# A decode block in one stream of weights: the pair sum and the last four row chunks of the down projection arranged differently

## The chip, the cores and the metric

One Trainium2 chip; the kernel runs on one of its cores. The metric is the device time of one execution in microseconds, the median of several runs. A profile is one profiled execution, in which the span runs from the first to the last instruction of the program.

## The reference

One decode step of a transformer block for 8 sequences: layer norm, attention over a window of W = 1024 cached positions (32 query heads, 4 key heads, head size 128), output projection and residual, then layer norm, a gated feed-forward part with gelu, and residual. All in float32, without casts.

```python
x = A_x                                             # 8 x 1 x 1024
h = x + _A_ref(_layernorm(x), A_k_cache, A_v_cache, A_wq, A_wo)
h2 = h + _B_ref(_layernorm(h), B_w_gate, B_w_up, B_w_down)
...
g = jnp.einsum("bsd,df->bsf", x, w_gate)            # 1024 -> 3584
u = jnp.einsum("bsd,df->bsf", x, w_up)
h = _gelu(g) * u
return jnp.einsum("bsf,fd->bsd", h, w_down)         # 3584 -> 1024
```

The down projection, the last einsum, is what the change touches: 3584 rows are 28 row chunks (q = 0 to 27) of 128 rows and 1024 columns, 512 KB each.

## The kernel before

All weights and the cache windows are laid out by the host as one flat array, in the order in which they are used, and read into one large buffer `w` of 128 partitions by transfers that SyncE issues (`load`, L102 to L104). Each transfer has a semaphore of its own, `loaded[i]`, on which TensorE waits before the first matmul that reads it. A place in `w` is written again when the matmuls that read it are done, so SyncE waits on TensorE's marks ahead of each issue. The list of loads: query weights (0, 1), keys (2, 3), values (4, 5), output weights (6, 7), gate and up weights (8 to 11), then the row chunks of the down projection in parts of 8, 8, 4, 4, 2 and 1 chunks (`DN_PARTS`, loads 12 to 17), and the last chunk 27 in two pieces: the first 192 columns of each quarter of 256 (`CUT`, load `tail`), then the other 64 of each (load `tail + 1`). That last piece, 128 rows of 1 KB, goes out as three transfers of 100, 20 and 8 partitions (`SHARES`, L329 to L331), all counted on one semaphore. All loads from part 3 on are issued in one go when the last up-projection matmul is done (L325 to L331).

Activations are kept transposed: a stationary operand of 128 rows by 32 columns holds the 8 sequences at every fourth column, and TensorE's 128 columns are used as four groups of 32, each of which writes 32 partitions of a PSUM bank. The activated hidden values are `at_[:, q, :]`.

The down projection runs over the row chunks (L357 to L396):

- Chunks 0 to 25 (`pairs`), L364: each is two matmuls of 512 columns. Up to chunk 19 (`SLOW`) they use two of the four groups; from 20 on even and odd chunks take different groups, so that four run side by side. They add up in bank 7, which then holds two halves, each as two partial sums on different partitions.
- VectorE copies bank 7 to `d1` (L371).
- Chunk 26, L378: four quarters of 256 columns, one to each group, in two pieces of 192 and 64 columns that start banks 0 and 1 (`fin`).
- The pair sum, L384: matmuls with the constant `add2` add the two partial sums of `d1` into the same quarters, in the same two pieces, on top of chunk 26.
- Chunk 27, L391: the same for the last chunk, each piece as its load arrives.
- VectorE adds the residual `h_sb` to each piece (L401, L404); SyncE stores the first (L407), ScalarE the second (L409).
- At the end SyncE waits for a count from ScalarE (`s_end`), clears the semaphores and waits for both stores.

The trace lists each float32 matmul twice, so L364 has 104 for 26 chunks of two.

Of the kernel before, what the change touches and what calls it, by code (L numbers as in the profile page):

```python
# [8 lines left out]
P = 128  # L9
B = 8  # L10
D = 1024
HQ, HKV, DH = 32, 4, 128
REP = HQ // HKV
DF = 3584
EPS = 1e-5
NC = D // P
NQ = 4
QW = D // NQ
# [4 lines left out]
GAP = 144  # L23
CUT = 192


ROUND = 3 * N * NC
PLACE = [0, HALF] * 5 + [0, ROUND]
DN_PARTS = (8, 8, 4, 4, 2, 1)
DN_AT = (2 * ROUND, 0, 8 * D, ROUND, ROUND + 4 * D, ROUND + 6 * D)  # L30

SHARES = ((0, 100), (100, 120), (120, 128))
LAST_AT = ROUND + 7 * D

SLOW = 20


class Engine:
# [39 lines left out]
def decode_block(nc, out, x, srcs, W):  # L78
# [3 lines left out]
    def sb(name, shape):  # L82
        return nc.alloc_sbuf_tensor(name, list(shape), F32).ap()

    first = nc.alloc_semaphore("first")
    pe = Engine(nc, nc.tensor, "pe")
    dve = Engine(nc, nc.vector, "dve")
# [4 lines left out]
    s_load = [nc.alloc_semaphore(f"s_load{i}") for i in range(len(srcs))]  # L92
    s_fin = nc.alloc_semaphore("s_fin")
    s_end = nc.alloc_semaphore("s_end")
    s_out = nc.alloc_semaphore("s_out")

    w = sb("w", [P, 2 * HALF])
    loaded = [(s, 16) for s in s_load]
    loaded[-1] = (s_load[-1], 16 * len(SHARES))
    tail = 12 + len(DN_PARTS)  # L100

    def load(i, at, size, *deps):  # L102
        sp.wait(*deps)
        nc.sync.dma_start(w[:, at:at + size], srcs[i]).then_inc(s_load[i], 16)  # L104
# [10 lines left out]
    t = pool(lambda e: e.memset(ident, 0.0))  # L115
# [8 lines left out]
    add2 = sb("add2", [P, 2, 32])  # L124
# [9 lines left out]
    def bank(i, n=1):  # L134
        return banks[:, i * N:(i + n) * N]
# [35 lines left out]
    for hf in range(2):  # L171
        q_ps = bank(4 + hf)
        for c in range(NC):
            for j in range(NQ):
                ins = pe(lambda e: e.matmul(  # L175
                    q_ps[32 * j:32 * j + 32, :], xt[:, c],
                    w[:, hf * HALF + c * SET + j * N:hf * HALF + c * SET + (j + 1) * N],
                    start=(c == 0), stop=(c == NC - 1)), loaded[hf], t_xt, inc=False)
# [3 lines left out]
    for hf in range(2):  # L182
        q_sb = sb(f"q{hf}", [P, N])
        t = dve(lambda e: e.tensor_scalar(q_sb, bank(4 + hf), scale, None, op0=ALU.mult), t_q[hf])  # L184
        qt = sb(f"qt{hf}", [P, N])
        t = dve(lambda e: e.transpose(qt, q_sb), t)
# [7 lines left out]
    t_s, t_p, share, t_share = [], [], [], []  # L194
    p_sb = [sb(f"p{hf}", [P, W]) for hf in range(2)]
    for hf in range(2):
        s_ps = bank(2 * hf, 2)
        k_t = w[:, hf * HALF:(hf + 1) * HALF].rearrange("p (s b k) -> p s b k", s=2, b=B)
        for b in range(HB):
            for k0 in range(0, W, N):  # L200
                for r in range(NQ):
                    s, half = divmod(r, 2)
                    at = 32 * b + 160 * half
                    ins = pe(lambda e: e.matmul(  # L204
                        s_ps[32 * r:32 * r + 32, k0:k0 + N], qz[hf][:, s, at:at + 32],
                        k_t[:, s, half * HB + b, k0:k0 + N],
                        start=(b == 0), stop=(b == HB - 1)), loaded[2 + hf], t_qz[hf], inc=False)
# [3 lines left out]
        t = dve(lambda e: e.tensor_reduce(out=nmax, in_=s_ps, axis=AX.X, op=ALU.max, negate=True), t_s[hf])  # L211
        tot = sb(f"tot{hf}", [P, 1])
        t = act(lambda e: e.activation(p_sb[hf], s_ps, AF.Exp, bias=nmax, accum_out=tot), t)  # L213
        t_p.append(t)
        rtot = sb(f"rtot{hf}", [P, 1])
        t = dve(lambda e: e.reciprocal(rtot, tot), t)
# [4 lines left out]
    t_o, o_sb, t_osb, t_ot = [], [], [], [None, None]  # L221
# [11 lines left out]
    for hf in range(2):  # L233
        pt = sb(f"pt{hf}", [P, KC, P])
        t_pt = []
        for h in range(2):
            pp = bank(6 + h).rearrange("p (c m) -> p c m", m=P)
            for i in range(KC // 2):
                c = h * KC // 2 + i
                ins = pe(lambda e: e.transpose(pp[:, i], p_sb[hf][:, c * P:(c + 1) * P], ident),  # L240
                         t_p[hf], t_id, free[h], inc=False)
            t = pe.mark(ins)
# [8 lines left out]
        for c in range(KC):  # L251
            for r in range(NQ):
                s, half = divmod(r, 2)
                ins = pe(lambda e: e.matmul(  # L254
                    o_ps[32 * r:32 * r + 32, :], pt[:, c, 32 * r:32 * r + 32],
                    v_t[:, s, c, half * HB:(half + 1) * HB, :],
                    start=(c == 0), stop=(c == KC - 1)), loaded[4 + hf], t_pt[2 * c // KC], t_qz[hf], inc=False)
# [3 lines left out]
        t = dve(lambda e: e.tensor_scalar(  # L261
            o_sb[hf], o_ps[:, 0:DH], share[hf][:, 0:1], None, op0=ALU.mult), t_o[hf], t_share[hf])
# [31 lines left out]
    t = pe.mark(ins)  # L294
# [7 lines left out]
    for k, nb in enumerate((NQ, DF // N - NQ)):  # L302
        pair = bank(2 + 2 * k, 2)
        t_g = []
        for s in range(2):
            i = 8 + 2 * k + s
            for c in range(NC):
                for j in range(nb):
                    at = PLACE[i] + (c * nb + j) * N
                    ins = pe(lambda e: e.matmul(  # L310
                        pair[32 * j:32 * j + 32, s * N:(s + 1) * N], ht[:, c], w[:, at:at + N],
                        start=(c == 0), stop=(c == NC - 1)), loaded[i], t_ht, t_p[1], t_osb[1], inc=False)
                if k == 0 and s == 1 and c == NC // 2 - 1:
                    t_half = pe.mark(ins)
            t_g.append(pe.mark(ins))
            if k == 0 and s == 0:
                load(10, PLACE[10], ROUND, t_g[0])
            elif k == 0:
                load(11, PLACE[11], ROUND, t_half)
                load(12, DN_AT[0], DN_PARTS[0] * D, t_g[1])  # L320
            elif s == 0:
                for i in range(1, 3):
                    load(12 + i, DN_AT[i], DN_PARTS[i] * D, t_g[0])
            else:
                for i in range(3, len(DN_PARTS)):  # L325
                    load(12 + i, DN_AT[i], DN_PARTS[i] * D, t_g[1])
                load(tail, LAST_AT, NQ * CUT)
                at = LAST_AT + NQ * CUT
                for p0, p1 in SHARES:  # L329
                    nc.sync.dma_start(w[p0:p1, at:at + D - NQ * CUT], srcs[tail + 1][p0:p1]).then_inc(  # L330
                        s_load[tail + 1], 16)  # L331
        rows = 32 * nb
        ge = sb(f"ge{k}", [P, N])
        t = act(lambda e: e.activation(ge[:rows], pair[:rows, 0:N], AF.Gelu_apprx_tanh), t_g[0])  # L334
        hm = sb(f"hm{k}", [P, N])
        t = dve(lambda e: e.tensor_mul(hm[:rows], ge[:rows], pair[:rows, N:2 * N]), t, t_g[1])  # L336
        if k == 0:
            t_at.append(dve(lambda e: e.transpose(at_[:, 0:16, :].rearrange("p c m -> p (c m)"), hm), t))
        else:
            hp = bank(6)[:, 0:4 * rows].rearrange("p (i m) -> p i m", i=4)  # L340
            for i in range(4):
                ins = pe(lambda e: e.transpose(hp[:, i], hm[:rows, i * P:(i + 1) * P], ident[:rows, :rows]),
                         t, t_ot[0], inc=False)
            t = pe.mark(ins)
            t_at.append(dve(lambda e: e.tensor_copy(
                at_[:, 16:28, :].rearrange("p (j i) m -> p i j m", j=nb),
                hp.rearrange("p i (j m) -> p i j m", j=nb)), t))
# [7 lines left out]
        of += [12 + i] * n  # L355

    d1_ps = bank(7)  # L357
    pairs = DF // P - 2
    started = set()
    for q in range(pairs):  # L360
        for ch in range(2):
            r = ch if q < SLOW else 2 * (q % 2) + ch
            at = where[q][0] + ch * N
            ins = pe(lambda e: e.matmul(  # L364
                d1_ps[32 * r:32 * r + 32, :], at_[:, q, :], w[:, at:at + N],
                start=(r not in started), stop=(q >= pairs - 2)),
                loaded[of[q]], t_at[0 if q < 16 else 1], t_ot[1], inc=False)
            started.add(r)
    t = pe.mark(ins)
    d1 = sb("d1", [P, N])  # L370
    t_d1 = dve(lambda e: e.tensor_copy(d1, d1_ps), t)  # L371

    fin = [(0, 0, CUT), (1, CUT, QW - CUT)]
    q = pairs
    for b, c0, n in fin:
        for j in range(NQ):
            at = where[q][0] + j * QW + c0
            pe(lambda e: e.matmul(  # L378
                bank(b)[32 * j:32 * j + 32, 0:n], at_[:, q, :], w[:, at:at + n],
                start=True, stop=False), loaded[of[q]], t_h, inc=False)  # L380
    for b, c0, n in fin:
        for j in range(NQ):
            at = (j % 2) * QW + c0
            pe(lambda e: e.matmul(  # L384
                bank(b)[32 * j:32 * j + 32, 0:n], add2[:, j // 2, :], d1[:, at:at + n],
                start=False, stop=False), t_d1, inc=False)
    o_fin = sb("o_fin", [P, QW])
    at = LAST_AT
    for i, (b, c0, n) in enumerate(fin):
        for j in range(NQ):  # L390
            ins = pe(lambda e: e.matmul(  # L391
                bank(b)[32 * j:32 * j + 32, 0:n], at_[:, pairs + 1, :], w[:, at:at + n],
                start=False, stop=True), loaded[tail + i], inc=False)
            at += n
        t = pe.mark(ins)
        fin[i] += (t,)  # L396
# [1 line left out]

    parts = [o_fin[:, c0:c0 + n] for b, c0, n, t in fin]
    b, c0, n, t = fin[0]  # L400
    t0 = dve(lambda e: e.tensor_add(parts[0], h_sb[:, c0:c0 + n], bank(b)[:, 0:n]), t)  # L401
    b, c0, n, t = fin[1]
    dve.wait(t)
    nc.vector.tensor_add(parts[1], h_sb[:, c0:c0 + n], bank(b)[:, 0:n]).then_inc(s_fin, 1)  # L404

    sp.wait(t0)
    nc.sync.dma_start(out[:, 0:CUT], parts[0]).then_inc(s_out, 16)  # L407
    nc.scalar.wait_ge(s_fin, 1).then_inc(s_end, 1)
    nc.scalar.dma_start(out[:, CUT:QW], parts[1]).then_inc(s_out, 16)  # L409

    nc.sync.wait_ge(s_end, 1).then_inc(s_end, -1)
    nc.sync.sem_clear(range(first.num, s_fin.num + 1))
    nc.sync.wait_ge(s_out, 32).then_inc(s_out, -32)

# [70 lines left out]
```

## Time and profile before

| | us |
|---|---|
| median of 3 runs (265.69 to 267.08) | 265.94 |
| the profiled execution's own time | 265.95 |
| its span, first to last instruction | 264.6 |

A page has the busy time of each engine, DMA by queue, and the chain of work that ended last. DMA queue q1 is that of SyncE's transfers, q10 that of ScalarE's, q8 fetches instructions, q14 tables. Besides the page the prediction reads the chain in order of time (start, duration, what), the timeline (start, duration, engine, line, operation, tiles, shape, count, and in brackets the idle time before it and what ended it), busy time by windows, and DMA by window. PE is TensorE's matmuls, PEld its loads of the stationary operand, DVE VectorE, ACT ScalarE, SPq and ACTq the queues of SyncE and ScalarE. In this execution:

| engine | busy us |
|---|---|
| TensorE, matmuls | 137.1 |
| TensorE, weight loads | 38.1 |
| VectorE | 24.2 |
| ScalarE | 10.2 |
| GpSimd | 2.7 |

### The profile page before, as it was taken

The page shows a single profiled execution, that of the slowest core. Times are in us where ns is not written, and L with a number is a line of the kernel's source. Part 1 is how long each engine was busy: PE and PEld are TensorE (multiplying, and loading weights), DVE is VectorE, ACT ScalarE, POOL GpSimd, SP SyncE. Part 2 cuts the span into 40 slices and gives each one's busy share as a digit, 9 for nine tenths or more (in the row PEclk, how much of TensorE's full clock was granted, in tenths as well). Part 3 has the DMA queues.
Part 4 walks back from the last instruction along what each step waited for, and adds up shares of the span by engine and source line. Part 5 has one row for each costly group of instructions (what it writes and reads, how often), then busy time and mean ns, then how long its engine had stood idle before and what let it go on. Part 6 is the DMA issues. An engine that isn't in the chain of part 4 may idle for free.

```text
span 264.6 us, 1990 instructions
## 1 busy us (share of the span) xinstructions
PE 137.1 (52%) x918; PEld 38.1 (14%) x918; DVE 24.2 (9%) x74; ACT 10.2 (4%) x14; POOL 2.7 (1%) x9
## 2 busy tenths in 40 slices
PE   0005706705806906807707708509409485689795
PEld 0001201101201301202102102102102021122131
DVE  1050200200110020300200000330000200010001
ACT  1020000000010020110000000020000000000000
POOL 4000000000000000000000000000000000000000
PEclk9999975955965895965975956956965959599999
DMA  8997999899999999998999899989999999999994
GB/s 317 480 466 327 475 475 428 367 466 475 406 396 466 468 396 416 456 475 357 448 457 456 367 446 458 456 386 436 458 411 446 394 468 411 423 421 411 426 417 135
DMA packets 3236, 111.44 MB, mean 421 GB/s; under 512 B 508, under 2 KB 796, under 8 KB 1052
## 3 DMA queue, kind: packets, MB, share of 16 engines
q1 hardware_dynamic: 3036, 111.25, 97.8%
q8 instruction: 7, 0.11, 0.2%
q10 hardware_dynamic: 192, 0.07, 0.1%
q14 instruction: 1, 0.01, 0.0%
HBM read 111.18 MB, written 0.13 MB: 421 GB/s over the span
## 4 chain that ended last, share of the span: by engine, by line
DMA 78%; PE 21%; SPq 0%; issue 0%; DVE 0%
DMA w<-weights 78%; PE banks L310 6%; PE banks L204 4%; PE banks L175 4%; PE banks L254 4%; PE banks L281 3%; SPq L104 0%; PE banks L378 0%; PE banks L384 0%; PE banks L391 0%; DVE o_fin L401 0%; DVE o_fin L404 0%; PE banks L225 0%
## 5 line engine op out<-in xcount | busy, mean ns | idle before, releaser
L310 PE MATMUL banks<-w,ln_t 128*32 128x512 f32 x224 | 37.4, 751 | 29.2 <-DMA w<-weights 29.2
L175 PE MATMUL banks<-w,ln_t 128*32 128x512 f32 x128 | 18.2, 734 | 33.2 <-DMA w<-weights 33.2
L204 PE MATMUL banks<-w,qz 128*32 128x512 f32 x128 | 19.3, 770 | 21.2 <-DMA w<-weights 21.2
L281 PE MATMUL banks<-w,ot 128*32 128x512 f32 x128 | 18.4, 741 | 19.2 <-DMA w<-weights 19.2
L254 PE MATMUL banks<-w,pt 128*32 128x512 f32 x128 | 18.0, 727 | 18.1 <-DMA w<-weights 18.1
L364 PE MATMUL banks<-w,at 128*32 128x512 f32 x104 | 20.3, 595 | 2.2 <-DMA w<-weights 2.1
L310 PEld LDWEIGHTS banks<-w,ln_t 128*32 128x32 f32 x224 | 9.2, 134 | 56.9 <-issue 34.2
L175 PEld LDWEIGHTS banks<-w,ln_t 128*32 128x32 f32 x128 | 4.7, 132 | 45.8 <-issue 34.5
L204 PEld LDWEIGHTS banks<-w,qz 128*32 128x32 f32 x128 | 5.3, 137 | 35.2 <-issue 35.2
L281 PEld LDWEIGHTS banks<-w,ot 128*32 128x32 f32 x128 | 5.0, 132 | 31.2 <-issue 31.2
L254 PEld LDWEIGHTS banks<-w,pt 128*32 128x32 f32 x128 | 4.9, 131 | 29.8 <-issue 29.8
L364 PEld LDWEIGHTS banks<-w,at 128*32 128x32 f32 x104 | 5.3, 109 | 16.5 <-issue 12.3
L336 DVE TENSOR_TENSOR hm<-ge,banks 128x512 f32<-128x512 f32 (+1 forms) x2 | 1.4, 686 | 60.3 <-PE banks L310 60.3
L211 DVE TENSOR_REDUCE nmax<-banks 128x1 f32<-128x1024 f32 x2 | 2.5, 1225 | 35.7 <-PE banks L204 35.7
L213 ACT ACTIVATE p<-banks,nmax 128x1024 f32<-128x1024 f32 x2 | 2.2, 1114 | 75.8 <-DVE nmax L211 75.8
L184 DVE TENSOR_SCALAR q<-banks 128x512 f32<-128x512 f32 x2 | 1.4, 692 | 32.3 <-PE banks L175 32.3
L261 DVE TENSOR_SCALAR o<-banks,share 128x128 f32<-128x128 f32 x2 | 0.7, 351 | 32.6 <-PE banks L254 32.6
L148 ACT ACTIVATE ln_sd<-ln_ve 32x1 f32<-32x1 f32 x2 | 0.4, 202 | 70.5 <-DVE ln_ve L146 70.5
L334 ACT ACTIVATE ge<-banks 128x512 f32<-128x512 f32 (+1 forms) x2 | 1.2, 595 | 48.2 <-PE banks L310 48.2
L371 DVE COPY d<-banks 128x512 f32<-128x512 f32 x1 | 0.7, 692 | 22.0 <-PE banks L364 22.0
L148 ACT ACT_TABLE_LOAD x2 | 2.6, 1283 | 1.7 <-DVE add L125 1.7
L228 DVE COPY ot<-banks 128x64 f32<-128x64 f32 x4 | 0.8, 262 | 18.4 <-PE banks L225 18.4
(55 smaller groups left out, 34.2 us busy)
## 6 DMA issues: line engine op xcount, KB each, us to landing
w<-weights SPq DMA_DIRECT2D x2, 6144.0 KB, 23.5
w<-weights SPq DMA_DIRECT2D x2, 4096.0 KB, 26.7
w<-weights SPq DMA_DIRECT2D x2, 2048.0 KB, 24.6
w<-weights SPq DMA_DIRECT2D x1, 1024.0 KB, 22.3
w<-weights SPq DMA_DIRECT2D x1, 512.0 KB, 23.6
w<-weights SPq DMA_DIRECT2D x1, 384.0 KB, 24.0
w<-weights SPq DMA_DIRECT2D x10, 29.6
w<-weights SPq DMA_DIRECT2D x1, 100.0 KB
```

The source lines that it names most:

```text
L148: t = act(lambda e: e.activation(sd, ve, AF.Sqrt), t_ve)
L175: ins = pe(lambda e: e.matmul(q_ps[32 * j:32 * j + 32, :], xt[:, c], w[:, hf * HALF + c * SET + j * N:hf * HALF + c * SET + (j + 1) * N], ...
L184: t = dve(lambda e: e.tensor_scalar(q_sb, bank(4 + hf), scale, None, op0=ALU.mult), t_q[hf])
L204: ins = pe(lambda e: e.matmul(s_ps[32 * r:32 * r + 32, k0:k0 + N], qz[hf][:, s, at:at + 32], k_t[:, s, half * HB + b, k0:k0 + N], start=(b ...
L211: t = dve(lambda e: e.tensor_reduce(out=nmax, in_=s_ps, axis=AX.X, op=ALU.max, negate=True), t_s[hf])
L213: t = act(lambda e: e.activation(p_sb[hf], s_ps, AF.Exp, bias=nmax, accum_out=tot), t)
L254: ins = pe(lambda e: e.matmul(o_ps[32 * r:32 * r + 32, :], pt[:, c, 32 * r:32 * r + 32], v_t[:, s, c, half * HB:(half + 1) * HB, :], start ...
L281: ins = pe(lambda e: e.matmul(y_ps[32 * r:32 * r + 32, :], ot[:, 2 * hf * REP + h + e_], w[:, at:at + N], start=(hf == 0 and h == 0), stop ...
L310: ins = pe(lambda e: e.matmul(pair[32 * j:32 * j + 32, s * N:(s + 1) * N], ht[:, c], w[:, at:at + N], start=(c == 0), stop=(c == NC - 1)), ...
L334: t = act(lambda e: e.activation(ge[:rows], pair[:rows, 0:N], AF.Gelu_apprx_tanh), t_g[0])
L336: t = dve(lambda e: e.tensor_mul(hm[:rows], ge[:rows], pair[:rows, N:2 * N]), t, t_g[1])
L364: ins = pe(lambda e: e.matmul(d1_ps[32 * r:32 * r + 32, :], at_[:, q, :], w[:, at:at + N], start=(r not in started), stop=(q >= pairs - 2) ...
```

## The change

Four things. The row chunks come in parts of 8, 8, 4, 3, 1, 2 and 1, and the single chunk of part 4, chunk 23 (`SHARED`), goes out as three transfers: partitions 0 to 79 as 16 blocks of 5 rows, 80 to 119 as 5 blocks of 8, 120 to 127 as 4 blocks of 2; on the host each block has one row of padding behind it. The last piece of chunk 27 is one transfer of 128 partitions again. Pairs run over chunks 0 to 23 only (`QUADS`); after the copy `d1` the pair sum comes first and starts bank 0, then chunks 24, 25 and 26 add to it as four quarters of 256 columns. VectorE adds bank 0 to the residual as `pre`, and chunk 27 alone is summed in banks 1 and 4, from zero; the last two adds of VectorE take `pre` in place of `h_sb`. GpSimd waits for `pre` at the end and counts on `s_end`, and SyncE waits for two counts.

```diff
-DN_PARTS = (8, 8, 4, 4, 2, 1)
-DN_AT = (2 * ROUND, 0, 8 * D, ROUND, ROUND + 4 * D, ROUND + 6 * D)
-
-SHARES = ((0, 100), (100, 120), (120, 128))
+DN_PARTS = (8, 8, 4, 3, 1, 2, 1)
+DN_AT = (2 * ROUND, 0, 8 * D, ROUND, ROUND + 3 * D, ROUND + 4 * D, ROUND + 6 * D)
 LAST_AT = ROUND + 7 * D
 
+SHARED = 4
+SHARES = ((16, 5), (5, 8), (4, 2))
+
 SLOW = 20
+QUADS = 24
...
                 for i in range(3, len(DN_PARTS)):
-                    load(12 + i, DN_AT[i], DN_PARTS[i] * D, t_g[1])
+                    if i != SHARED:
+                        load(12 + i, DN_AT[i], DN_PARTS[i] * D, t_g[1])
+                        continue
+                    for (n, each), (p0, src) in zip(SHARES, srcs[12 + i]):
+                        nc.sync.dma_start(w[p0:p0 + n * each, DN_AT[i]:DN_AT[i] + D], src).then_inc(
+                            s_load[12 + i], 16)
                 load(tail, LAST_AT, NQ * CUT)
-                at = LAST_AT + NQ * CUT
-                for p0, p1 in SHARES:
-                    nc.sync.dma_start(w[p0:p1, at:at + D - NQ * CUT], srcs[tail + 1][p0:p1]).then_inc(
-                        s_load[tail + 1], 16)
+                load(tail + 1, LAST_AT + NQ * CUT, D - NQ * CUT)
...
-    pairs = DF // P - 2
     started = set()
-    for q in range(pairs):
+    for q in range(QUADS):
...
-    fin = [(0, 0, CUT), (1, CUT, QW - CUT)]
-    q = pairs
-    for b, c0, n in fin:
+    for j in range(NQ):
+        pe(lambda e: e.matmul(
+            bank(0)[32 * j:32 * j + 32, 0:QW], add2[:, j // 2, :], d1[:, (j % 2) * QW:(j % 2) * QW + QW],
+            start=True, stop=False), t_d1, inc=False)
+    rows = DF // P
+    for q in range(QUADS, rows - 1):
         for j in range(NQ):
-            at = where[q][0] + j * QW + c0
-            pe(lambda e: e.matmul(
-                bank(b)[32 * j:32 * j + 32, 0:n], at_[:, q, :], w[:, at:at + n],
-                start=True, stop=False), loaded[of[q]], t_h, inc=False)
-    for b, c0, n in fin:
-        for j in range(NQ):
-            at = (j % 2) * QW + c0
-            pe(lambda e: e.matmul(
-                bank(b)[32 * j:32 * j + 32, 0:n], add2[:, j // 2, :], d1[:, at:at + n],
-                start=False, stop=False), t_d1, inc=False)
+            at = where[q][0] + j * QW
+            ins = pe(lambda e: e.matmul(
+                bank(0)[32 * j:32 * j + 32, 0:QW], at_[:, q, :], w[:, at:at + QW],
+                start=False, stop=(q == rows - 2)), loaded[of[q]], inc=False)
+    t = pe.mark(ins)
+    pre = sb("pre", [P, QW])
+    t_pre = dve(lambda e: e.tensor_add(pre, h_sb, bank(0)[:, 0:QW]), t)
+
+    fin = [(1, 0, CUT), (4, CUT, QW - CUT)]
...
             ins = pe(lambda e: e.matmul(
-                bank(b)[32 * j:32 * j + 32, 0:n], at_[:, pairs + 1, :], w[:, at:at + n],
-                start=False, stop=True), loaded[tail + i], inc=False)
+                bank(b)[32 * j:32 * j + 32, 0:n], at_[:, rows - 1, :], w[:, at:at + n],
+                start=True, stop=True), loaded[tail + i], t_osb[0], t_p[0], inc=False)
...
-    t0 = dve(lambda e: e.tensor_add(parts[0], h_sb[:, c0:c0 + n], bank(b)[:, 0:n]), t)
+    t0 = dve(lambda e: e.tensor_add(parts[0], pre[:, c0:c0 + n], bank(b)[:, 0:n]), t, t_pre)
...
-    nc.vector.tensor_add(parts[1], h_sb[:, c0:c0 + n], bank(b)[:, 0:n]).then_inc(s_fin, 1)
+    nc.vector.tensor_add(parts[1], pre[:, c0:c0 + n], bank(b)[:, 0:n]).then_inc(s_fin, 1)
...
-    nc.sync.wait_ge(s_end, 1).then_inc(s_end, -1)
+    nc.gpsimd.wait_ge(*t_pre).then_inc(s_end, 1)
+    nc.sync.wait_ge(s_end, 2).then_inc(s_end, -2)
...
-    for a in loads:
+    for i, a in enumerate(loads):
...
+        if i == 12 + SHARED:
+
+            p0, parts = 0, []
+            for n, each in SHARES:
+                block = np.zeros((n, each + 1, two.shape[1]), np.float32)
+                block[:, :each] = two[p0:p0 + n * each].reshape(n, each, -1)
+                parts.append((f0, p0, n, each, a.shape[1]))
+                flat.append(block.reshape(-1))
+                f0 += block.size
+                p0 += n * each
+            places.append(parts)
+            continue
```

More of the change, by code (lines that the diff above doesn't have):

```diff
@@ L98, in decode_block @@
     loaded = [(s, 16) for s in s_load]
-    loaded[-1] = (s_load[-1], 16 * len(SHARES))
+    loaded[12 + SHARED] = (s_load[12 + SHARED], 16 * len(SHARES))
     tail = 12 + len(DN_PARTS)
@@ L365, in decode_block @@
                 d1_ps[32 * r:32 * r + 32, :], at_[:, q, :], w[:, at:at + N],
-                start=(r not in started), stop=(q >= pairs - 2)),
+                start=(r not in started), stop=(q >= QUADS - 2)),
                 loaded[of[q]], t_at[0 if q < 16 else 1], t_ot[1], inc=False)
@@ L476 @@
     flat = aps["weights"]
-    srcs = [
-        flat[f0:f0 + P * (size + GAP)].rearrange("(p n) -> p n", p=P)[:, 0:size]
-        for f0, size in places
-    ]
+    srcs = []
+    for place in places:
+        if isinstance(place, tuple):
+            f0, size = place
+            srcs.append(flat[f0:f0 + P * (size + GAP)].rearrange("(p n) -> p n", p=P)[:, 0:size])
+        else:
+            srcs.append([
+                (p0, flat[f0:f0 + n * (each + 1) * (size + GAP)].rearrange(
+                    "(a b n) -> a b n", a=n, b=each + 1)[:, 0:each, 0:size])
+                for f0, p0, n, each, size in place
+            ])
     decode_block(nc, out, aps["x"], srcs, W)
```

## The prediction

> **What bounds the kernel now.** I read the page's totals and its chain of work first.
>
> ```profile
> span 264.6 us, 1990 instructions
> HBM read 111.18 MB, written 0.13 MB: 421 GB/s over the span
> q8 instruction: 7, 0.11, 0.2%
> DMA 78%; PE 21%; SPq 0%; issue 0%; DVE 0%
> ```
>
> The kernel is one long load of 111 MB, so nothing ahead of the last transfers matters unless it makes the queue run dry; the change touches only the last 2 MB of it. So the end is what to read, in order of time:
>
> ```profile
> 237.18 23.60 DMA w<-weights
> 260.78 0.04 issue
> 260.82 0.64 PE banks L378 x16
> 261.47 0.44 PE banks L384 x16
> 261.90 0.41 PE banks L391 x8
> 262.31 0.02 issue
> 262.33 0.35 DVE o_fin L401
> 262.69 0.13 DVE o_fin L404
> ```
>
> From 260.82 on the chain is not DMA: TensorE does row chunk 26 (L378), the pair sum (L384) and the last chunk (L391) back to back, then VectorE adds twice. The timeline shows how close the transfers are behind it:
>
> ```profile
> 256.55 0.21 PEld L364 LDWEIGHTS banks<-w,at 128*32 128x32 f32 x6 [0.22 <-issue]
> ...
> 258.36 1.74 PE L364 MATMUL banks<-w,at 128*32 128x512 f32 x10
> 259.04 0.16 PEld L364 LDWEIGHTS banks<-w,at 128*32 128x32 f32 x8 [0.99 <-DMA w<-weights]
> 260.17 0.69 DVE L371 COPY d<-banks 128x512 f32<-128x512 f32 x1 [21.95 <-PE banks L364]
> 260.82 0.64 PE L378 MATMUL banks<-w,at 128*32 128x192 f32 x16 [0.72 <-DMA w<-weights]
> 261.28 0.62 PE L384 MATMUL banks<-d,add 128*32 128x192 f32 x16
> 261.73 0.76 PE L391 MATMUL banks<-w,at 128*32 128x192 f32 x16
> 262.18 0.16 PEld L391 LDWEIGHTS banks<-w,at 128*32 128x32 f32 x8 [0.29 <-DMA w<-weights]
> 262.61 0.21 DVE L404 TENSOR_TENSOR o_fin<-h_sb,banks 128x64 f32<-128x64 f32 x1
> 262.93 0.35 ACTq L409 DMA_DIRECT2D out<-o_fin  x1
> ```
>
> The last load lands just before 262.18 (TensorE waited 0.29 us for it), its sums are there by 262.61, VectorE ends at 262.82, and the store goes out at 262.93. So **two paths end together**: sums on TensorE (to 262.31, then 0.35 and 0.13 on VectorE) and the last landing at 262.14. An edit must shorten both.
>
> Why the last landing is where it is stands in the busy time by windows (after the clock, the last two columns are the DMA share and GB/s):
>
> ```profile
> 250.00:256.00 6.00, 6.00 (x30) 1.63 (x28) 0.00 (x0) 0.00 (x0) 0.00 (x0) 1.00 0.97 412
> 259.25:260.00 0.75, 0.75 (x8) 0.00 (x0) 0.00 (x0) 0.00 (x0) 0.00 (x0) 1.00 0.76 198
> 260.00:260.75 0.75, 0.10 (x4) 0.00 (x0) 0.58 (x1) 0.00 (x0) 0.00 (x0) 1.00 0.45 158
> 260.75:261.25 0.50, 0.43 (x16) 0.36 (x19) 0.11 (x1) 0.00 (x0) 0.00 (x0) 1.00 0.14 51
> 261.25:261.50 0.25, 0.25 (x20) 0.22 (x16) 0.00 (x0) 0.00 (x0) 0.00 (x0) 1.00 0.04 12
> ```
>
> A share of 0.45 is 7 of 16 DMA engines, 0.14 is 2.2, 0.04 less than one. The engines do not end together: over half are done by 260.0, the last at about 261.4. The rest is uneven because each takes its own fixed rows of every transfer, and some lost time earlier. The page counts seven instruction fetches; one of them, and the one table load, seen alone by their queues' shares of a 2 us window:
>
> ```profile
> q8 instruction: 1, 0.02, 3.0%
> q14 instruction: 1, 0.01, 1.0%
> ```
>
> 3.0% of 16 engines over 2 us is 0.96 us on one engine, 1.0% is 0.32 us. The spread at the end is 2 us, not six or seven fetches long, so I read them as falling on different engines: some six are late by about 1 us, one by 0.3. Which is late the trace does not name, except for the last one. From 260.82 to 261.5 the DMA view counts:
>
> ```profile
> DMA packets 26, 0.03 MB, mean 42 GB/s; under 512 B 8, under 2 KB 21, under 8 KB 26
> ```
>
> Of 26 packets 8 are counts of a few bytes, 21-8 = 13 are 1 KB rows and 5 are 3 KB rows. The 1 KB rows are the last load, which goes out as 100, 20 and 8 rows; in tenths, tenths and eighths this is 10+2+1 = 13 rows for each of the first eight engines, 12 for two, none for the last six. So the last 13 packets are all those of **one late engine among the first eight**, and the five 3 KB rows belong to late engines that have no share.
>
> [...]
>
> **The change part by part.** Units first. 412 GB/s over 16 engines is 25.75 GB/s each: a 4 KB row costs 0.159 us. 12 GB/s over 0.25 us is three 1 KB rows after 261.25; 13 rows from 260.82 to 261.4 are 0.045 us each.
>
> Rows shared out. Chunk 23 becomes its own transfer in three: 16x5, 5x8 and 4x2 rows. Read like 100, 20 and 8, engines 0 to 3 get 15 rows, engine 4 gets 13, engines 5 to 15 get 5, where an even split gives 8. In turn the last load goes back to 8 rows of 1 KB each. Against before:
> - the late ones of the last six: 3 rows fewer (-0.48), 8 small rows more (+0.36). The last 3 KB rows ended at about 261.2 (two engines at work in 260.75 to 261.25), so they end at 261.08. From last packet to use was 0.5 us for the 3 KB load (261.2 to 261.73) and 0.74 for the three-part one (261.4 to 262.14): they land at 261.6 to 261.8.
> - the late one of the first eight: 5 small rows fewer (-0.22), and -0.48, +0.80 or +1.11 with 5, 13 or 15 rows: it ends at 260.7, 262.0 or 262.3.
> - the engine with the table load, if among the first eight, stood 0.64 us ahead of that one (0.96-0.32), so 260.8; with 15 rows 261.65, landing at 262.15 to 262.4.
>
> In the stretch from 259.25 to 260.00 each busy engine moved 198/(16x0.76) = 16.3 GB/s against 412/(16x0.97) = 26.5, so 0.29 us of it were lost. Nothing in the trace says to what, so an engine working later may or may not lose it: 0 to 0.29 us less in each number of the last two lines, and the same 0 to 0.29 more if the odd split crowds the engines; I take 0.15 less.
>
> TensorE. The pair matmuls end with chunk 23 instead of 25, so the copy d (0.69 us) no longer waits for the load at 259.04. The old chunks 20 to 23 were done before that (the last two matmuls began at 258.36 and take 0.6: 258.96). Chunk 23 was in hand by then; up to seven more rows on one engine, 1.11 us, still lie under 1.7 us of pair matmuls between 256.55 and 258.3, so I cost its own transfer at nothing; were that cover gone, d would slip by the same amount. Now the copy runs 259.02 to 259.71. **Behind it on TensorE's queue stand** the four-quarter sum (8 matmuls) and then chunks 24, 25 and 26, 8 each, although 24 and 25 land between 0.48 us before and 1.1 us after the 259.0 of now and could have gone first. The pitch is that from L378 to L384 to L391: 260.82, 261.28, 261.73, so 0.455 us for 256 columns of four quarters. Four such steps from 259.75 end at 261.57; with 0.15 us for the last to drain, the new add of VectorE, pre, starts at 261.7. It is 256 wide: between 0.35 (192 wide) and 0.69 (512 wide), by columns 0.43. It ends at 262.15. Only then can the add of the first part run (0.35) and the second behind it (0.13 more): VectorE ends at 262.6 instead of 262.82. The count of matmuls falls from 152 to 144 here (104+16+16+16 to 96+8+24+16).
>
> The last chunk in banks of its own: its 16 matmuls start from zero instead of adding; same number and width. With PE free at 261.57, the first part is done by 262.1, before pre. Banks 1 and 4 are long read; no wait ends late.
>
> SyncE's queue. One transfer more is issued at 236.33:
>
> ```profile
> 236.33 1.75 SPq L104 DMA_DIRECT2D w<-weights  x4
> 238.13 1.08 SPq L330 DMA_DIRECT2D w<-weights  x3
> ```
>
> Seven issues took 2.9 us, eight take 3.3 and end at 239.6, with the engines at 0.97 share on earlier loads until 256. Hidden by 15 us and more; nothing.
>
> GpSimd waits for pre at the end and SyncE for a second count. Pre is there at 262.15; SyncE then waits for the stores, until 264.6 anyway. Hidden by 2 us; no row shows what a waiting GpSimd costs around the span, so 0 to 0.2 us more, taken as 0.
>
> **Sum.** The profiled execution took 265.95 us (span 264.6), the median is 265.94: the same, so differences go onto the median. If no landing comes after about 262.1, VectorE's chain sets the end, 0.22 us earlier. 265.94-0.22 = **265.7**. A gain from the loads alone (0.35 to 0.5 us) is cut off by the sum behind d.
>
> **The rivals.**
> *The late engine of the first eight is one of 0 to 3.* It gets seven rows more and ends at 262.3, less 0 to 0.29; landing 0.5 to 0.74 later is 262.5 to 263.05 against 262.14: the end moves by +0.37 to +0.9, **266.5**. It decides from about ten rows on: 260.7+5x0.159 = 261.5, landing at 262.0 to 262.25, when VectorE comes free for the second part. For it: four of eight engines, and one late engine there is certain by the 13 packets. Against it: it may be any of eight. With engine 4, 0.3 us earlier, it is 266.0 to 266.5. This is the case that ends slower.
>
> *The split moves no ends.* If the parts of a shared transfer do not fall as read, or crowd one another as in the slow stretch, the late six end with 8 small rows more, 261.2+0.36, landing at 262.05 to 262.3; the end moves by -0.1 to +0.15: **265.95**. Against it speak the 13 packets. [...]
>
> *The sum is not what is late.* If TensorE takes the 256 wide steps faster, or the copy starts earlier, the late six decide (261.6): 265.45. This is the low end of the forecast.
>
> **How the numbers follow.** Forecast, late engine at 4 to 7 and d's chain at the end: four of eight, less a fifth for the rival about the split, 0.42; 265.45 to 266.0 (265.7), with engine 4 at the upper end. Late engine at 0 to 3: 0.38, 266.3 to 266.85; a little less than half, since the slow stretch can take back its price. The split that moves nothing: 0.20, 265.8 to 266.1. The range from 265.3 to 266.75 leaves out the ends of each, some 0.15. About 0.5%, 1.33 us, is what a measurement of this kernel can tell from no change; every case lies inside it. For faster by more, all of the spread of 2 us would have to go and TensorE's chain with it: 0.04. For slower by more, the late engine's seven rows and a crowded split together: 0.05. Within: 0.91.
>
> **What would show it.** Right: copy d starting near 259.0 and 8 sum matmuls right behind it; pre ending near 262.1; VectorE's first add started by pre, not by TensorE; the store near 262.7. In the windows the share falls later but more steeply. Wrong: the first add released by TensorE with pre long done, and a wait for a load at the second part of the last chunk near 262.6 or later (the slow rival); a slope of the share from 259.25 as before (the split moved nothing); TensorE waiting for chunk 23 after 258. A change of over 1 us anywhere ahead of 236 us would make all of this beside the point.

## The result, and the profile after

| | before | the change |
|---|---|---|
| median of 7 runs, us | 266.01 (265.69 to 267.08) | 268.56 (267.80 to 268.96) |
| profiled execution, us | 265.95 | 268.63 |
| its span, us | 264.6 | 267.3 |

The ratio is 1.0084, 95% interval 1.0062 to 1.0106: slower by about 2.5 us, where 0.24 us less was forecast (265.7) and 266.75 was the upper end. The runs of the kernel before lie in two groups, at 265.7 to 266.1 and near 267.05 us, and its ranges take in both. The page after, totals and the shares of the chain:

```profile
span 267.3 us, 1978 instructions
HBM read 111.18 MB, written 0.13 MB: 416 GB/s over the span
q8 instruction: 7, 0.11, 0.2%
DMA 77%; PE 20%; SPq 1%; issue 0%; DVE 0%
```

The same bytes, the same seven fetches, 2.7 us more of span. The end of the chain, in order of time:

```profile
240.33 23.97 DMA w<-weights
264.29 0.04 issue
264.34 0.69 PE banks L396 x16
265.03 0.34 DVE o_fin L406
265.36 0.13 DVE o_fin L409
```

Before, a load led to 260.78 and sums took over. Now a load leads to 264.29, the first piece of the last chunk, and only that chunk's sums and the two adds are behind it. This points to the loads. The timeline says the same further up (start, duration, engine, line, operation; the idle time before it in brackets):

```profile
259.88 0.14 PEld L367 LDWEIGHTS banks<-w,at 128*32 128x32 f32 x4 [1.73 <-DMA w<-weights]
260.98 0.69 DVE L374 COPY d<-banks 128x512 f32<-128x512 f32 x1 [22.50 <-PE banks L367]
261.73 0.64 PE L377 MATMUL banks<-d,add 128*32 128x256 f32 x8 [0.80 <-DVE d L374]
263.38 0.64 PE L384 MATMUL banks<-w,at 128*32 128x256 f32 x8 [0.15 <-DMA w<-weights]
264.09 0.42 DVE L389 TENSOR_TENSOR pre<-h_sb,banks 128x256 f32<-128x256 f32 x1 [2.41 <-PE banks L384]
265.60 0.35 ACTq L414 DMA_DIRECT2D out<-o_fin  x1
```

TensorE waits for chunk 23, the shared one, until 259.88 (its weight loads stand idle 1.73 us, its matmuls 0.82), and for chunk 26 until 263.38, where before it had that at 260.82. Where the loads lose the time shows in the windows (the last two columns are the DMA share and GB/s). The first line is from before, the others from the change:

```profile
253.00:258.00 5.00, 5.00 (x34) 1.51 (x32) 0.00 (x0) 0.00 (x0) 0.00 (x0) 1.00 0.96 399
246.00:252.00 6.00, 5.40 (x26) 1.54 (x28) 0.00 (x0) 0.00 (x0) 0.00 (x0) 1.00 1.00 425
253.00:258.00 5.00, 4.94 (x28) 1.21 (x26) 0.00 (x0) 0.00 (x0) 0.00 (x0) 1.00 1.03 216
263.25:264.25 1.00, 0.64 (x8) 0.16 (x8) 0.16 (x1) 0.00 (x0) 0.00 (x0) 1.00 0.07 26
```

From 253 to 258 the DMA engines count as busy throughout (1.03) and together they move 216 GB/s instead of 399. That is 5 us x (399-216) = 0.92 MB not moved, 2.3 us of loading at 399: nearly the whole loss. A busy share does not tell at what speed an engine is busy; only beside the GB/s does it.

### The profile page after: what moved, and what is told of

It is laid out like the page before. It is cut to its first block, busy times and chain, and to the rows that moved or that the text cites. A ratio compares the mean times of both kernels' runs of the same rounds, so it can differ in the third digit from the quotient of the medians.

```text
span 267.3 us, 1978 instructions
## 1 busy us (share of the span) xinstructions
PE 138.1 (52%) x910; PEld 37.7 (14%) x910; DVE 24.6 (9%) x75; ACT 10.2 (4%) x14; POOL 2.7 (1%) x9
## 4 chain that ended last, share of the span: by engine, by line
DMA 77%; PE 20%; SPq 1%; issue 0%; DVE 0%
DMA w<-weights 77%; PE banks L312 5%; PE banks L177 4%; PE banks L256 4%; PE banks L283 3%; PE banks L206 3%; SPq L332 1%; SPq L106 1%; PE banks L396 0%; DVE o_fin L406 0%; DVE o_fin L409 0%; PE banks L227 0%
## 5 line engine op out<-in xcount | busy, mean ns | idle before, releaser
L312 PE MATMUL banks<-w,ln_t 128*32 128x512 f32 x224 | 37.3, 747 | 29.2 <-DMA w<-weights 29.2
L177 PE MATMUL banks<-w,ln_t 128*32 128x512 f32 x128 | 19.1, 763 | 32.7 <-DMA w<-weights 32.7
L206 PE MATMUL banks<-w,qz 128*32 128x512 f32 x128 | 18.3, 736 | 20.5 <-DMA w<-weights 20.5
L256 PE MATMUL banks<-w,pt 128*32 128x512 f32 x128 | 18.8, 753 | 19.0 <-DMA w<-weights 19.0
L283 PE MATMUL banks<-w,ot 128*32 128x512 f32 x128 | 17.6, 710 | 20.1 <-DMA w<-weights 20.1
L290 DVE COPY y_sb<-banks 128x512 f32<-128x512 f32 x1 | 0.7, 692 | 19.3 <-PE banks L283 19.3
```

The source lines that it names most:

```text
L177: ins = pe(lambda e: e.matmul(q_ps[32 * j:32 * j + 32, :], xt[:, c], w[:, hf * HALF + c * SET + j * N:hf * HALF + c * SET + (j + 1) * N], ...
L206: ins = pe(lambda e: e.matmul(s_ps[32 * r:32 * r + 32, k0:k0 + N], qz[hf][:, s, at:at + 32], k_t[:, s, half * HB + b, k0:k0 + N], start=(b ...
L256: ins = pe(lambda e: e.matmul(o_ps[32 * r:32 * r + 32, :], pt[:, c, 32 * r:32 * r + 32], v_t[:, s, c, half * HB:(half + 1) * HB, :], start ...
L283: ins = pe(lambda e: e.matmul(y_ps[32 * r:32 * r + 32, :], ot[:, 2 * hf * REP + h + e_], w[:, at:at + N], start=(hf == 0 and h == 0), stop ...
L312: ins = pe(lambda e: e.matmul(pair[32 * j:32 * j + 32, s * N:(s + 1) * N], ht[:, c], w[:, at:at + N], start=(c == 0), stop=(c == NC - 1)), ...
```

## The experiments

Each ratio is against the kernel before on the same chip.

**Chunk 23 as 16 blocks of 8 rows** takes away the unequal counts.

```diff
-SHARES = ((16, 5), (5, 8), (4, 2))
+SHARES = ((16, 8),)
```

> The change with chunk 23 as one transfer of 16 blocks of 8 rows (its source still in padded blocks): every engine gets 8 rows. The three theories: R, the odd split puts the rows of several engines onto the same partitions, so that all loads from 253 to 258 us run at half their rate; U, it is only the count, 15 rows on some engines; B, it is the padded blocks in the source. R and U: the slow stretch goes, about 400 GB/s from 253 to 258, 265.7 to 266.3 us. B: the stretch stays, 268 us or more.

267.95 us (267.88 to 268.08), ratio 1.0069 (1.0048 to 1.0090). The stretch stays:

```profile
253.00:258.00 5.00, 5.00 (x28) 1.32 (x26) 0.00 (x0) 0.00 (x0) 0.00 (x0) 1.00 1.04 248
```

U falls: with 8 rows for every engine, by the count of shares, the loads still run at 248 GB/s. R as I had put it, several engines on the same partitions by an odd split, did not say that even blocks would be slow either.

**Blocks of 5 and of 3 rows**, by the same count again 8 for each engine.

```diff
-SHARES = ((16, 5), (5, 8), (4, 2))
+SHARES = ((16, 5), (16, 3))
```

> The change with chunk 23 as two transfers, 16 blocks of 5 rows (partitions 0 to 79) and 16 blocks of 3 (80 to 127): every engine has 8 rows again, but in odd places. U: like an even split, 265.7 to 266.3 us. R: a slow stretch of 1 to 2 us is left, about half the rate while the 512 KB go out, 266.8 to 268 us.

268.04 us (267.73 to 268.11), ratio 1.0069 (1.0048 to 1.0091); 242 GB/s from 253 to 258. The same as even blocks. By the medians both lie 0.5 to 0.6 us under the change itself, and 0.3 to 0.4 under the run below that has the loads of the change and was taken beside them (268.36). The intervals of the ratios overlap, so this is about what the counts 15, 13 and 5 can cost; the split as such costs about 2.

**The sums of the change with the loads of before.**

```diff
-DN_PARTS = (8, 8, 4, 3, 1, 2, 1)
+DN_PARTS = (8, 8, 4, 4, 2, 1)
...
-                load(tail + 1, LAST_AT + NQ * CUT, D - NQ * CUT)
+                at = LAST_AT + NQ * CUT
+                for p0, p1 in SHARES:
+                    nc.sync.dma_start(w[p0:p1, at:at + D - NQ * CUT], srcs[tail + 1][p0:p1]).then_inc(
+                        s_load[tail + 1], 16)
```

> The loads of before, the sums of the change (pair sum after chunk 23, pre, banks 1 and 4, GpSimd's wait). R, U and B lay all of the loss on the loads: 265.5 to 266.0 us here, the first add of VectorE released by pre or by the last loads. S, that the sum ahead of chunks 24 to 26 is what makes the change late: 267 us or more.

266.06 us, ratio 1.0005 (0.9979 to 1.0032). S falls, and the new order of sums can be read by itself, here in its timeline:

```profile
259.14 0.69 DVE L372 COPY d<-banks 128x512 f32<-128x512 f32 x1 [20.64 <-PE banks L365]
259.89 0.64 PE L375 MATMUL banks<-d,add 128*32 128x256 f32 x8 [0.83 <-DVE d L372]
260.34 1.48 PE L382 MATMUL banks<-w,at 128*32 128x256 f32 x24
261.70 0.64 PE L394 MATMUL banks<-w,at 128*32 128x192 f32 x16
261.89 0.42 DVE L387 TENSOR_TENSOR pre<-h_sb,banks 128x256 f32<-128x256 f32 x1 [2.06 <-PE banks L382]
262.38 0.35 DVE L404 TENSOR_TENSOR o_fin<-pre,banks 128x192 f32<-128x192 f32 x1
262.97 0.36 ACTq L412 DMA_DIRECT2D out<-o_fin  x1
```

TensorE stands idle 0.83 us until d is there; sum and chunks 24 to 26 then run in steps of 0.45 us with no wait for a load, pre follows, and the last store goes out at 262.97, against 262.93 before. The first add begins at 262.38, behind pre (262.31) and behind the last chunk's sums (262.34); the two end so close together that the trace does not tell which one it waited for.

**The loads of the change with the sums of before** (the part of the program from bank 7 to the last store put back).

> The loads of the change (chunk 23 in three transfers, last piece whole), the sums of before. R, U and B: all of the loss is here, 268.3 to 269 us, the slow stretch from 253 to 258 as in the change. S: 266 to 266.5 us.

268.36 us (268.06 to 268.77), ratio 1.0080 (1.0053 to 1.0106), 224 GB/s from 253 to 258. All of the loss is in the loads.

**Chunk 23 as one ordinary load**, all else as in the change.

```diff
-                    if i != SHARED:
-                        load(12 + i, DN_AT[i], DN_PARTS[i] * D, t_g[1])
-                        continue
-                    for (n, each), (p0, src) in zip(SHARES, srcs[12 + i]):
-                        nc.sync.dma_start(w[p0:p0 + n * each, DN_AT[i]:DN_AT[i] + D], src).then_inc(
-                            s_load[12 + i], 16)
+                    load(12 + i, DN_AT[i], DN_PARTS[i] * D, t_g[1])
```

> The change with chunk 23 as one ordinary load of 128 rows, no blocks and no padding; its last piece is whole too. The even blocks of the first run were as slow as the odd ones, so U has fallen. Left are P, the place: engine by engine the split writes partitions in an order in which several engines meet at the same part of the buffer, and B, the padded source. Both: about 410 GB/s from 253 to 258 us and 265.6 to 266.2 us. If it is slow, it is neither, but a load of 512 KB of its own.

265.96 us, ratio 0.9985 (0.9963 to 1.0007):

```profile
253.00:258.00 5.00, 5.00 (x34) 1.45 (x32) 0.00 (x0) 0.00 (x0) 0.00 (x0) 1.00 1.00 409
```

The same 128 rows to the same 128 partitions as in the first experiment, by the count of shares again 8 for each of 16 engines, at 409 GB/s in place of 248. What is left is which rows an engine gets and in what order, or the padded source.

**Two ordinary loads of 80 and 48 partitions** take the padding out and leave the split.

```diff
-                    if i != SHARED:
+                    if i != 4:
                         load(12 + i, DN_AT[i], DN_PARTS[i] * D, t_g[1])
                         continue
-                    for (n, each), (p0, src) in zip(SHARES, srcs[12 + i]):
-                        nc.sync.dma_start(w[p0:p0 + n * each, DN_AT[i]:DN_AT[i] + D], src).then_inc(
+                    for p0, p1 in ((0, 80), (80, 128)):
+                        nc.sync.dma_start(w[p0:p1, DN_AT[i]:DN_AT[i] + D], srcs[12 + i][p0:p1]).then_inc(
                             s_load[12 + i], 16)
```

> As the run before, but chunk 23 as two ordinary loads of partitions 0 to 79 and 80 to 127, rows one behind the other in the source as in every other load. 5 and 3 rows for each engine. P: as slow as the blocks of 5 and 3 were, 250 GB/s from 253 to 258 us and 267.4 to 268.2 us. B: no slow stretch, 265.6 to 266.2 us.

267.93 us (267.62 to 268.43), ratio 1.0061 (1.0042 to 1.0079):

```profile
253.00:258.00 5.00, 5.00 (x30) 1.31 (x26) 0.00 (x0) 0.00 (x0) 0.00 (x0) 1.00 1.03 266
```

B falls: no padding, the source in the order of all other loads, and slow.

Which rows are slow can be read too, since a trace lists each DMA packet, here one row of a load, with its size and time. The median times of the rows that start between 253 and 258:

| row | load | the change | 80 and 48 partitions | chunk 23 plain |
|---|---|---|---|---|
| 12 KB | part 3, ordinary | 0.91 us | 0.80 us | 0.465 us |
| 4 KB | mostly chunk 23 | 0.31 us | 0.27 us | 0.16 us |
| 8 KB | chunks 24 and 25, ordinary | 0.63 us | 0.51 us | 0.31 us |

The rows of the ordinary loads on either side take 1.6 to 2 times as long, as the rows of chunk 23 itself do.

**The disputed thing by itself: 64 partitions, low or in the middle.** One load of 2 MB, part 1, with 64 rows, all loads else plain, and the sums of the change. Both kernels leave out the other 64 rows of this part, so they read 2 MB less and their sums are not those of the block. The second run has 32 and 96 in place of 0 and 64.

```diff
-                    load(12 + i, DN_AT[i], DN_PARTS[i] * D, t_g[0])
+                    if i == 1:
+                        sp.wait(t_g[0])
+                        nc.sync.dma_start(
+                            w[0:0+64, DN_AT[1]:DN_AT[1] + 8 * D], srcs[13][0:0+64]).then_inc(s_load[13], 16)
+                    else:
+                        load(12 + i, DN_AT[i], DN_PARTS[i] * D, t_g[0])
```

> Plain loads and the sums of the change; of part 1 (chunks 8 to 15) only partitions 0 to 63 are loaded, 2 MB, 4 rows on each engine; the other half of these rows holds older weights. Beside it the same with partitions 32 to 95. P: the rate depends on where the 64 partitions lie. [...] B: no difference, both 410 GB/s and about 261 us.

> As the run before with partitions 32 to 95 in place of 0 to 63. P: 380 to 420 GB/s while the 2 MB load, and 4 to 5 us shorter than it, about 261 us. B: the same as it.

272.08 us and 263.29 us, one run each. The windows of the stretch around that load, partitions 0 to 63 first:

```profile
236.00:248.00 12.00, 8.11 (x42) 2.14 (x36) 1.24 (x2) 0.00 (x0) 0.00 (x0) 1.00 0.95 194
```

and partitions 32 to 95:

```profile
236.00:248.00 12.00, 11.20 (x57) 3.31 (x56) 1.24 (x2) 0.00 (x0) 0.00 (x0) 1.00 0.98 418
```

Same bytes, same number of rows, same source layout; 194 GB/s against 418. For 64 rows the place decides, so P stands; why it decides, neither run shows. The size I had expected, an estimate that no run had shown, was too small: 8.8 us apart, not 4 to 5. In neither run do the loads alone set the time; the second has TensorE at the pair matmuls without a break from 237.38 on, so it takes 263.29 us where about 261 was expected:

```profile
237.38 19.06 PE banks L367 x92
```

The loads themselves end at 256.3 and 264.6, 8.2 us apart. The slow stretch is 12 us or more for a load of 2 MB that at half of 418 GB/s would need 10, and the ordinary load behind it is slowed with it: from 246 to 248 its rows of 16 KB take 1.28 us each in the first run and 0.61 in the second. That both are under way at once because the engines are a microsecond or two out of step, some still in the slow load while others are not, is argued and not shown.

What the two runs show, they show for a load of 64 rows. That chunk 23 in parts is slow for the same reason is the reading that fits, but it is not shown by itself: no trace names the engine that writes a row, and for chunk 23 the order in which the engines read the source is a rival that no run takes out (in the two runs with 64 rows that order is the same, 32 rows further on).

**Plain loads with the sums of the change.**

```diff
-DN_PARTS = (8, 8, 4, 3, 1, 2, 1)
+DN_PARTS = (8, 8, 4, 4, 2, 1)
```

with the blocks and their padding taken out as well.

> The sums of the change, all loads plain: chunk 23 back in part 3, last piece whole. P has held in the runs so far. It says that the last piece in 100, 20 and 8 rows of before clashes a little too (the slow stretch from 259.25 to 260 us) and that taking it away is worth 0 to 0.3 us; TensorE's chain behind the copy d takes it back: 265.7 to 266.1 us, first add of VectorE started by pre.

266.03 us, ratio 0.9999 (0.9980 to 1.0019). Its windows at the end answer to the open slow stretch of before:

```profile
259.25:260.00 0.75, 0.04 (x4) 0.05 (x7) 0.65 (x1) 0.00 (x0) 0.00 (x0) 1.00 0.54 209
```

209/(16x0.54) is 24.2 GB/s for each busy engine, where before had 16.3. So the stretch with the last piece in 100, 20 and 8 partitions was slow too. The rows say the same: from 259.25 to 260.00 those of 1, 3 and 4 KB take 0.067, 0.16 and 0.23 us before and 0.046, 0.12 and 0.16 here.

**The kernel before with its last piece whole.**

```diff
-                for p0, p1 in SHARES:
-                    nc.sync.dma_start(w[p0:p1, at:at + D - NQ * CUT], srcs[tail + 1][p0:p1]).then_inc(
-                        s_load[tail + 1], 16)
+                load(tail + 1, LAST_AT + NQ * CUT, D - NQ * CUT)
```

> The kernel before with its last piece whole, nothing else changed. The late engines have 8 small rows more, the late one among the first eight 5 fewer, and the clash is gone. P: 265.6 to 266.2 us, no change to speak of. If the 100, 20 and 8 rows really evened out the engines, 266.3 to 266.6 us.

266.35 us, ratio 1.0004 (0.9984 to 1.0024). The median says little: six of the 12 runs took 265.64 to 265.77 us and six 266.93 to 267.39, and it lies between. The lower six are 0.18 us below the lower 23 of the 35 runs of before beside them (medians 265.72 and 265.90), so nothing speaks for an uneven piece that evened out the engines, which was to cost 0.3 us and more when taken away. The profiled run is one of the upper six and shows TensorE late, not the loads: its granted clock was 0.57 from 248 to 252, against 1.00 there before, and copy d began at 261.99 instead of 260.17.

**Sums earlier, loads plain.** The pairs end with chunk 19, chunks 20 to 23 come as quarters ahead of the pair sum, so that TensorE has work until d is there.

```diff
-SLOW = 20
-QUADS = 24
+SLOW = 16
+QUADS = 20
...
-    for j in range(NQ):
-        pe(lambda e: e.matmul(
-            bank(0)[32 * j:32 * j + 32, 0:QW], add2[:, j // 2, :], d1[:, (j % 2) * QW:(j % 2) * QW + QW],
-            start=True, stop=False), t_d1, inc=False)
...
     for q in range(QUADS, rows - 1):
+        for j in range(NQ * (q == 24)):
+            pe(lambda e: e.matmul(
+                bank(0)[32 * j:32 * j + 32, 0:QW], add2[:, j // 2, :], d1[:, (j % 2) * QW:(j % 2) * QW + QW],
+                start=False, stop=False), t_d1, inc=False)
...
-                start=False, stop=(q == rows - 2)), loaded[of[q]], inc=False)
+                start=(q == QUADS), stop=(q == rows - 2)), loaded[of[q]], t_h, inc=False)
```

> All loads plain, but the pairs end with chunk 19 (chunks 16 to 19 already four side by side), chunks 20 to 23 are added as quarters, then the pair sum, then 24 to 26. The copy d then runs about 256 us under loads, TensorE has only chunk 26 left when it lands and pre is ready about 261.8 us. The end hangs on the last landing alone: the last store at 262.6 to 262.8 us in place of 262.9 to 263.0, 265.5 to 265.9 us.

265.61 us (265.46 to 265.76), ratio 0.9976 (0.9962 to 0.9990): a little faster than before, and faster than the change. Its timeline:

```profile
260.56 0.64 PE L379 MATMUL banks<-w,at 128*32 128x256 f32 x8 [0.17 <-DMA w<-weights]
261.27 0.42 DVE L384 TENSOR_TENSOR pre<-h_sb,banks 128x256 f32<-128x256 f32 x1 [4.72 <-PE banks L379]
261.48 0.64 PE L391 MATMUL banks<-w,at 128*32 128x192 f32 x16 [0.28 <-DMA w<-weights]
262.15 0.35 DVE L401 TENSOR_TENSOR o_fin<-pre,banks 128x192 f32<-128x192 f32 x1 [0.46 <-PE banks L391]
262.75 0.36 ACTq L409 DMA_DIRECT2D out<-o_fin  x1
```

pre waits for chunk 26 and nothing else, each later step for its load, and the last store goes out 0.18 us before that of before. Part of the ratio is that none of the 12 runs is near 267 us, where 12 of the 35 of before are; against the other 23 (265.90) the gain is 0.29 us. Copy d runs at 255.86 here, over 4 us earlier than before, so a TensorE that falls behind as in the run above would have cover; that this is why no run is near 267 is argued and not shown.

**The same with the last piece in 100, 20 and 8 partitions** (the loads of before).

> The same order of sums with the loads of before, the last piece in 100, 20 and 8 rows. If these evened out the engines, the last landing is 0.1 us ahead of the whole piece and the time 265.4 to 265.8 us; if they only clash, no better than the run before.

265.92 us (265.76 to 266.17), ratio 0.9987 (0.9972 to 1.0001). Not better than the plain loads but worse, by 0.31 us between the medians, though the two profiled runs both took 265.76. With the sums out of the way the uneven last piece does not pay; and without the whole piece the new order of sums gains nothing on those 23 runs of before (265.90).

## Why the prediction was wrong

**The step that failed** is the price of a shared row. The prediction took "a 4 KB row costs 0.159 us" from the rate of ordinary loads, summed rows engine by engine, and cost chunk 23's own transfer at nothing. Split in any way tried, the rows of chunk 23 do not run at that rate, and neither do the loads beside them: 242 to 266 GB/s over 5 us with equal counts, 216 and 224 with those of the change, 409 for one load of 128. A 4 KB row took 0.31 us in the change. Chunk 23 was to be in hand by 258.3 and came at 259.88; TensorE waiting for it is one of the signs of being wrong that the prediction names. That is the loss, about 2 us with equal counts (267.93 to 268.04 against 265.96) and 2.5 with 15, 13 and 5.

**The sign of it stood in the trace of before.** The prediction saw 16.3 GB/s for a busy engine in the 0.75 us where the 100, 20 and 8 rows ran beside other loads, said that nothing in the trace told to what the rest was lost, and carried it as 0 to 0.29 us. It was the one place at its end where that kernel splits a load oddly. Scaled by the bytes it would have been a warning, 4 x 0.29 = 1.2 us: 128 KB there, 512 KB in the change, and in the middle of the stream with all engines at work, not at its end.

**The rival that the split moves nothing** named crowding as in that stretch. The working allows 0 to 0.29 us for it, and the rival lets the end move by at most 0.15. The rows did run slower (4 KB in 0.31 us, against 0.16 with chunk 23 plain), and the size was several times larger: about 2 us. What holds them up, no run shows.

**The sums** went nearly as worked out, seen in the loads of before: copy d at 259.14 (worked out 259.02), the sum right behind it, steps of 0.45 us, pre from 261.89 to 262.31 (to 262.15). The gain of 0.22 us from it did not come: d is 0.12 us later than worked out, the steps behind it lose another 0.1, VectorE ends at 262.86 instead of 262.6, and store and time are those of before (1.0005, 0.9979 to 1.0032). That TensorE waits for d with chunks 24 and 25 behind it was right. The order that avoids this gained only together with a whole last piece (265.61, against 265.92 with the split one).

**The late engine among the first four.** The prediction's reading of the last 13 rows as one engine's holds: in the packets of before they follow one another from 260.83 to 261.39, each beginning as the one before it ends, with a packet of 4 bytes behind the 10th, the 12th and the 13th. How many engines share a transfer was read right too: the page counts 508 packets under 512 B before and 521 in the change, and the 13 more are 25 (16+5+4) for chunk 23 and 16 for a whole last piece in place of 28 (10+10+8). That the engines with 15 rows are among the eight with 13, on which the chances of four in eight rest, no run shows. The counts 15, 13 and 5 cost 0.3 to 0.6 us over equal ones by the medians, with intervals that overlap; that this is near the price of that rival is no proof of it. In the change one engine's worth of work is left alone at the end, share 0.07 from 263.25 to 264.25, which is 1.1 of 16. Its packets, followed back, put it at the first row behind chunk 23 only at 259.03, which fits an engine with 15 rows; how many rows it had and whether it was late before, they do not say, and this stays open.

**GpSimd's wait, banks 1 and 4, the padded blocks and SyncE's queue** were costed at nothing; the first two are in the sums run at 1.0005. The issues ended at 241.2 (239.6 worked out): the three block transfers took 2.36 us to issue, where the three pieces of before took 1.08. Loads were in hand until 264, so this cost nothing that shows. The padding is not what makes blocks slow, since two plain loads were slow too (266 GB/s, against 242 and 248 with blocks).

## What to carry to other kernels

Equal row counts on the DMA engines did not make equal speed here: with 8 rows for each, by the count of shares, chunk 23 in parts ran at 242 to 266 GB/s with the loads beside it, and as one load of 128 partitions at 409. Before costing a row at the average rate, look in the profile for a stretch where a load of that very shape ran, and read its GB/s per busy engine. And where a sum waits for a copy, put the work that is ready in front of it on that queue.

## What the runs showed of the hardware

Over the 12 us around a load of 64 partitions the rate was 418 GB/s when they were 32 to 95 and 194 when they were 0 to 63. Over the 5 us around a load of 128 rows it was 409 GB/s when they went out as one load of 128, and 248 as 16 blocks of 8 rows to the same partitions, which by the count of shares is 8 rows on each of 16 engines in both. In the packets of before, followed from end to start from 230 to 250 us, there are 16 sequences, in each of which 8 rows of a whole load are followed by one packet of 4 bytes; which engine writes which partition, and so why the rates differ, no run shows. Rows of an ordinary load that ran beside the shared rows took up to twice their time, 0.91 us against 0.465 for 12 KB.
